# The gate by pairs of batches: tiles of 128 tokens, contractions of 128 rows, and its weights split in the MLP

## The chip, the cores and the metric

One core of one Trainium2 chip runs the whole program. The metric is device time in microseconds of one execution, given as the median of several. The core has a matrix engine (TensorE, PE here; PEld is its weight load), VectorE (DVE), ScalarE (ACT), GpSimd (POOL), and SyncE (SP), which issues most DMAs. Each engine runs its instructions in the order in which they were written.

## The reference

Three parts, in float32, with 4 batches, 448 tokens, 12 heads of 64, model width 768:

```python
x = attention(rmsnorm(q), rmsnorm(k), v)            # [4, 448, 768]
x = x + relu(layernorm(x) * g @ w_ch1) @ w_ch2      # hidden width 3072
h = relu(x @ w_in)                                  # [4, 448, 1024]
u, v = h[..., :512], h[..., 512:]
v_n = (v - mean(v)) / sqrt(var(v) + 1e-6)
v_s = einsum('ts,bsd->btd', w_spatial, v_n) + b_spatial[None, :, None]
out = (u * v_s) @ w_out                             # [4, 448, 768]
```

The last five lines are "the gate" below; `w_spatial` is 448x448.

## The kernel before

Large products are made in three float32r matmuls: each operand is split into a rounded part (`hi`) and the rest (`lo`), and `THREE` names the pairs hi*hi, hi*lo, lo*hi. A split costs one copy (ACT or DVE) and one subtraction (POOL or DVE).

Each part of the kernel first lists its operations with `op(n, engine, us, fn, r, w, new)`: an intended place `n`, an estimate of the time, what is read and written, and the ring of buffers that is used. `arrange` then plays the list through with these estimates and writes the instructions out in the order in which they would start; that order is fixed at build time.

Attention comes first. Then the MLP runs 24 slices `u` of the hidden width over 4 batches: `ph` (18 matmuls), `pm` (18 matmuls), the latter one step behind; ACT and DVE make `h` from `ph`, DVE adds `pm` to `y`. The slices' weights come as 64-bit numbers into a raw slot (`wraw`), are converted to float32 into `wc` by ACT and four DVE operations (`plan_conv`), and split by ACT and POOL into `ws` (`plan_parts`). Between them stand sixteen "gate" pieces: `w_in` and `w_out` are converted in the same way, and stored to DRAM from `wc` as plain float32 (`win_dram`, `wout_dram`).

The gate follows at about 999 us, batch by batch, in `plan_gate`:

- `gv`: per batch four tiles of 112 tokens, each 18 matmuls that stream 512 columns of the weights of v against the tokens of `ys` (the split input). ACT applies relu, DVE takes mean and variance, makes the reciprocal root in eleven small steps for all four tiles (`rsqrt_steps`), scales and rounds; POOL makes the rest (`gvs`).
- `gu`: four groups of 128 columns of u, 18 matmuls each over 448 tokens.
- `gs`: four groups, each contracting over the 448 tokens in four tiles of 112 rows, 12 matmuls.
- DVE adds the bias and multiplies by u, ACT and POOL split the result (`gg`).
- `gp`, after each second batch (`plan_out`): 14 row tiles of 128 in two halves of 12 matmuls, copied by ACT (`go`) and stored.

The gate's weights are loaded and split there: v's at the MLP's end (`plan_win`), u's and `w_out` in the first batch; `w_spatial` is loaded, transposed by PE in 16 small matmuls (`psp`) and split. The inputs of batches 1 to 3 go through DRAM (`y_dram`), since `ys` has one buffer.

Of the kernel before, what the change touches and what calls it, by code (L numbers as in the profile page):

```python
# [34 lines left out]
def f32(ap):  # L35
    return ap.bitcast(F32)
# [3 lines left out]
def attention_mlp_gated(ctx, tc, q, k, v, g_q, g_k, g_ln, w1, w2, w_in, w_sp, b_sp, w_out, out):  # L40
# [19 lines left out]
    win_dram = dram.tile([DM, 2 * DG], F32, name="win_dram")  # L60
    wout_dram = dram.tile([DG, DM], F32, name="wout_dram")
# [5 lines left out]
    gl_c = const.tile([P, NK], F32, name="gl_c")  # L67


    def rsqrt_steps(y, t, a):  # L70
# [13 lines left out]
        return steps  # L84

# [80 lines left out]
    def plan_parts(i, n, since=()):  # L166
# [15 lines left out]
        if kind == "gate":  # L182
            dma(n, src.shape[1] / 2, lambda: nc.sync.dma_start(u, pl["c"]), r=[c])
# [10 lines left out]
    TURN = 0.19  # L194

# [592 lines left out]
    def plan_gate(gp, W, ys, b, n):  # L788

        st = {}  # L790
        vn, uu = {}, {}
        cols = slice(b % 2 * S, (b % 2 + 1) * S)
        yr = [f"ys{b}_{kk}" for kk in range(NK)]

        def v_pe(c):
            pv = st["pv", c] = ps["s"].tile([P, 512], F32, tag="s", name=f"gv{b}_{c}")
            for kk in range(NK):
                for m, (a, e) in enumerate(THREE):
                    nc.tensor.matmul(  # L799
                        pv[:CP, :],  # L800
                        ys[b][:, a, kk, c * CP : (c + 1) * CP],
                        W["v", kk][:, e],
# [4 lines left out]
        def v_act(c):  # L807
            vn[c] = gp["vr"].tile([CP, DG], F32, tag="vr", name=f"vr{b}_{c}")
            nc.scalar.activation(vn[c], st["pv", c][:CP, :], AF.Relu)

        def v_stats(c):
            if c == 0:
                st["mv"] = gp["small"].tile([CP, NCH, 2], F32, tag="gmv", name=f"gmv{b}")
            s6 = gp["small"].tile([CP, 6], F32, tag="g6", name=f"g6{b}_{c}")
            nc.vector.bn_stats(s6, vn[c])
            nc.vector.bn_aggr(st["mv"][:, c], s6)

        def v_rstd(z):
# [14 lines left out]

        def v_hi(c):
            if c == 0:
                st["vs"] = gp["vs"].tile([CP, NCH, 2, DG], F32R, tag="xn", name=f"gvs{b}")
            nc.vector.tensor_copy(st["vs"][:, c, 0], vn[c])

        def v_lo(c):
            nc.gpsimd.tensor_tensor(st["vs"][:, c, 1], vn[c], f32(st["vs"][:, c, 0]), op=ALU.subtract)  # L840

        for c in range(NCH):
            o = f"{b}_{c}"
            op(n, "PE", 3.84, lambda c=c: v_pe(c), r=yr + [f"win_v{kk}" for kk in range(NK)], w=["gv" + o], new="s")
            op(n + 1, "ACT", 0.48, lambda c=c: v_act(c), r=["gv" + o], w=["vr" + o], new="vr")
            op(n + 1, "DVE", 0.7, lambda c=c: v_stats(c), r=["vr" + o], w=["mv" + o])
        for z in range(11):
            op(n + 3, "DVE", 0.07, lambda z=z: v_rstd(z), r=[f"mv{b}_{c}" for c in range(NCH)], w=[f"rstd{b}"])
        for c in range(NCH):
            o = f"{b}_{c}"  # L850
            op(n + 4, "DVE", 0.34, lambda c=c: v_norm(c), r=[f"rstd{b}"], w=["vr" + o])
            if c == 0:
                op(n + 4, "DVE", 0.34, lambda: v_hi(0), r=["vr" + o], w=[f"vs{b}", "vs" + o], new="vs")
            else:
                op(n + 4, "DVE", 0.34, lambda c=c: v_hi(c), r=["vr" + o, f"vs{b}"], w=["vs" + o])
            op(n + 4, "POOL", 1.23, lambda c=c: v_lo(c), r=["vr" + o, f"vs{b}"], w=["vs" + o])

        def u_pe(g):
            pu = st["pu", g] = ps["t"].tile([P, 512], F32, tag="t", name=f"gu{b}_{g}")
            for kk in range(NK):  # L860
                for m, (a, e) in enumerate(THREE):
                    nc.tensor.matmul(  # L862
                        pu[:, :S],
                        W["u", kk][:, a, g * P : (g + 1) * P],
                        ys[b][:, e, kk, :],
                        start=(kk == 0 and m == 0),
                        stop=(kk == NK - 1 and m == 2),
                    )

        def u_act(g):  # L870
            uu[g] = gp["u"].tile([P, S], F32, tag="gu", name=f"u{b}_{g}")
            nc.scalar.activation(uu[g], st["pu", g][:, :S], AF.Relu)

        for g in range(NG):
            o = f"{b}_{g}"
            op(n + 8, "PE", 3.37, lambda g=g: u_pe(g), r=yr + [f"win_u{kk}" for kk in range(NK)], w=["gu" + o], new="t")
            op(n + 9, "ACT", 0.424, lambda g=g: u_act(g), r=["gu" + o], w=["u" + o], new="u")

        def s_pe(g):
            pg = st["pg", g] = ps["o"].tile([P, 512], F32, tag="o", name=f"gs{b}_{g}")  # L880
            for c in range(NCH):
                for m, (a, e) in enumerate(THREE):
                    nc.tensor.matmul(  # L883
                        pg[:, :S],
                        st["vs"][:, c, a, g * P : (g + 1) * P],
                        W["sp"][:, e, c, :],
                        start=(c == 0 and m == 0),
                        stop=(c == NCH - 1 and m == 2),
                    )

        def s_add(g):
            st["t", g] = gp["t"].tile([P, S], F32, tag="gt", name=f"gt{b}_{g}")
            nc.vector.tensor_tensor(
                st["t", g], st["pg", g][:, :S], W["b"].rearrange("p c i -> p (c i)"), op=ALU.add
            )

        def s_gate(g):
            nc.vector.tensor_tensor(st["t", g], st["t", g], uu[g], op=ALU.mult)

        def s_hi(g):  # L900
            if b % 2 == 0:
                gt[g] = gp["g"].tile([P, 2, 2 * S], F32R, tag="gg", name=f"gg{b}_{g}")
            act_copy(gt[g][:, 0, cols], st["t", g])

        def s_lo(g):
            eng = nc.vector if b == B - 1 else nc.gpsimd
            eng.tensor_tensor(gt[g][:, 1, cols], st["t", g], f32(gt[g][:, 0, cols]), op=ALU.subtract)

        for g in range(NG):
            o = f"{b}_{g}"  # L910
            r = [f"vs{b}"] + [f"vs{b}_{c}" for c in range(NCH)] + [f"wsp{c}" for c in range(NCH)]
            op(n + 16, "PE", 2.25, lambda g=g: s_pe(g), r=r, w=["gs" + o], new="o")
            op(n + 17, "DVE", 0.535, lambda g=g: s_add(g), r=["gs" + o, "bsp"], w=["gt" + o], new="gt")
            op(n + 17, "DVE", 0.535, lambda g=g: s_gate(g), r=["u" + o], w=["gt" + o])
            both = f"gg{b // 2 * 2}_{g}"
            r, w, new = (["gt" + o, both], [f"gg{b}_{g}_"], None) if b % 2 else (["gt" + o], [both, f"gg{b}_{g}_"], "gg")
            op(n + 17, "ACT", 0.46, lambda g=g: s_hi(g), r=r, w=w, new=new)
# [361 lines left out]
```

## Time and profile before

| | |
|---|---|
| median of 3 runs | 1229.29 us (1228.19 to 1230.41) |
| the profiled execution | 1229.24 us |
| its span | 1227.5 us |
| PE busy | 1198.8 us, 98% of the span |
| DVE, ACT, POOL busy | 794.9, 451.3, 325.1 us |
| MLP and gate | about 302 to 999 us, and 999 to 1224 us |

Busy times are means over stages with different limits. A stage is read from its chain of waits: the pieces of work that ended last there, in order of time, each released by the one before it. Times inside the trace count from the start of the span.

### The profile page before, as it was taken

The numbers are of one execution on the slowest core, as the hardware profiler recorded it, in microseconds if no ns is written. First come the engines' busy times: TensorE is split into PE (matmuls) and PEld (weight loads), VectorE is DVE, ScalarE is ACT, GpSimd is POOL, SyncE is SP. The second block draws the span as 40 slices with busy tenths as digits, with TensorE's granted clock in tenths as the row PEclk, the third lists the DMA queues.
The fourth block names the chain that finished last, engine by engine and source line by source line (L and its number), as shares of the span: only waits on it lengthen the run. The fifth ranks groups of instructions, "written<-read, shape, count | busy, mean of one in ns | idle before, by whom it ended". The sixth has DMA issues, their size and how long they took to land.

```text
span 1227.5 us, 16696 instructions
## 1 busy us (share of the span) xinstructions
PE 1198.8 (98%) x6528; PEld 1020.5 (83%) x6528; DVE 794.9 (65%) x1436; ACT 451.3 (37%) x910; POOL 325.1 (26%) x266
## 2 busy tenths in 40 slices
PE   3999999999999999999999999999999999999998
PEld 1556656566899999999999999999999989889898
DVE  5889998977898656464747484855535578452250
ACT  2888888887422212131212122221212222122112
POOL 4764767525111102020202011110201115212120
PEclk9999999999999999999999999999999999999999
DMA  4312112111214231231313141402100063011103
GB/s 100 80 54 77 53 46 73 61 42 42 77 54 153 69 104 54 101 93 62 112 44 112 52 156 51 154 26 78 53 26 26 26 227 113 23 46 52 39 1 90
DMA packets 50861, 89.00 MB, mean 73 GB/s; under 512 B 3952, under 2 KB 39152, under 8 KB 50016
## 3 DMA queue, kind: packets, MB, share of 16 engines
q1 hardware_dynamic: 50352, 83.82, 22.5%
q10 hardware_dynamic: 432, 4.13, 0.8%
q8 instruction: 51, 0.84, 0.3%
q14 instruction: 26, 0.21, 0.1%
HBM read 73.58 MB, written 14.35 MB: 72 GB/s over the span
## 4 chain that ended last, share of the span: by engine, by line
PE 89%; DVE 7%; DMA 2%; ACT 1%; issue 0%; POOL 0%; SPq 0%; DVEq 0%
PE ph L705 28%; PE pm L728 28%; PE s L475 5%; PE gp L930 5%; PE gu L862 5%; PE gv L799 4%; PE po L525 4%; PE t L508 4%; PE gs L883 3%; DVE nmx L481 2%; DMA win_ru<-win_dram 1%; PE pk L452 1%; PE pq L452 1%; PE pxT L580 1%; DVE PT L518 1%; PE px L559 1%
## 5 line engine op out<-in xcount | busy, mean ns | idle before, releaser
L728 PE MATMUL pm<-h,ws 128*128 128x448 f32 x1728 | 361.6, 362 | 0.0
L705 PE MATMUL ph<-xn,ws 128*128 128x448 f32 x1728 | 361.1, 362 | 0.0
L728 PEld LDWEIGHTS pm<-h,ws 128*128 128x128 f32 x1728 | 323.7, 187 | 22.4 <-issue 0.7
L705 PEld LDWEIGHTS ph<-xn,ws 128*128 128x128 f32 x1728 | 323.8, 187 | 21.8 <-DVE y L736 0.2
L180 POOL TENSOR_TENSOR ws<-wc,ws 128x768 fp32r<-128x768 f32 x48 | 96.5, 2009 | 574.8 <-ACT ws L101 561.9
L736 DVE TENSOR_TENSOR y<-pm,y 128x448 f32<-128x448 f32 x318 | 175.9, 613 | 76.7 <-PE pm L728 76.7
L715 ACT ACTIVATE h<-ph 128x448 fp32r<-128x448 f32 x96 | 51.9, 541 | 267.1 <-PE ph L705 259.7
L720 DVE SCALAR_TENSOR_TENSOR h<-ph,h 128x448 fp32r<-128x448 f32 x96 | 59.5, 620 | 125.7 <-ACT h L715 124.6
L485 ACT ACTIVATE P<-s,nmx 112x448 f32<-112x448 f32 x192 | 119.2, 635 | 30.7 <-DVE nmx L481 30.4
L481 DVE TENSOR_REDUCE nmx<-s 112x2 f32<-112x896 f32 x96 | 101.0, 1080 | 18.7 <-PE s L475 18.1
L91 ACT ACTIVATE wc<-wr 128x768 f32<-128x768 f32 (+1 forms) x64 | 55.2, 865 | 139.3 <-POOL ws L180 45.8
L475 PE MATMUL s<-kT,qT 64*112 64x448 f32 x384 | 88.3, 581 | 0.6 <-ACT qT L461 0.6
L508 PE MATMUL t<-ident,P 112*112 112x112 f32 x768 | 85.4, 260 | 1.7 <-ACT P L485 1.0
L101 ACT ACTIVATE ws<-wc 128x768 fp32r<-128x768 f32 x48 | 40.6, 845 | 113.1 <-PE ph L705 97.2
L508 PEld LDWEIGHTS t<-ident,P 112*112 112x112 f32 x768 | 75.9, 133 | 5.0 <-ACT P L485 4.1
L525 PE MATMUL po<-PT,vr 112*64 112x448 f32 x384 | 77.5, 545 | 0.0
L94 DVE SCALAR_TENSOR_TENSOR wc<-wr,wc 128x768 int32<-128x768 int32 (+1 forms) x64 | 69.2, 1081 | 1.6
L95 DVE SCALAR_TENSOR_TENSOR wc<-wr,wc 128x768 uint32<-128x768 uint32 (+1 forms) x64 | 67.6, 1057 | 1.1
L92 DVE TENSOR_SCALAR wc<-wc 128x768 f32<-128x768 f32 (+1 forms) x64 | 37.6, 587 | 46.3 <-ACT wc L91 46.3
L799 PE MATMUL gv<-winv,ys 128*112 128x512 f32 x288 | 67.2, 393 | 0.0
L475 PEld LDWEIGHTS s<-kT,qT 64*112 64x112 f32 x384 | 31.5, 179 | 41.6 <-issue 23.4
L525 PEld LDWEIGHTS po<-PT,vr 112*64 112x64 f32 x384 | 25.4, 136 | 48.5 <-issue 38.4
(167 smaller groups left out, 1267.5 us busy)
## 6 DMA issues: line engine op xcount, KB each, us to landing
wr<-in_moe_w_ch_dram SPq DMA_DIRECT2D x48, 768.0 KB, 4.4
wr<-in_moe_w_in_dram SPq DMA_DIRECT2D x12, 512.0 KB, 3.8
vr<-in_v_dram SPq DMA_DIRECT2D x24, 224.0 KB, 2.7
kr<-in_k_dram SPq DMA_DIRECT2D x11, 448.0 KB, 4.0
qr<-in_q_dram SPq DMA_DIRECT2D x11, 448.0 KB, 4.5
y_dram<-y ACTq DMA_DIRECT2D x3, 1344.0 KB, 9.0
yl<-y_dram SPq DMA_DIRECT2D x3, 1344.0 KB, 7.2
win_dram<-wc SPq DMA_DIRECT2D x12, 256.0 KB, 4.7
```

The lines of the kernel that those rows point to most:

```text
L94: lambda: v.scalar_tensor_tensor(ci, hi, -0x40000000, ci, op0=ALU.bitwise_and, op1=ALU.bitwise_or),
L95: lambda: v.scalar_tensor_tensor(cu, lo.bitcast(U32), 29, cu, op0=ALU.logical_shift_right, op1=ALU.bitwise_or),
L180: nc.gpsimd.tensor_tensor(t[:, 1], pl["c"], f32(t[:, 0]), op=ALU.subtract)
L475: nc.tensor.matmul(p[:CP, j, :S], pr["qT"][rows, c * CP : (c + 1) * CP], pr["kT"][rows], start=True, stop=True)
L481: nc.vector.tensor_reduce(t, pr["s", c][:CP, :, :S], axis=AX.X, op=ALU.max, negate=True)
L485: nc.scalar.activation(t, pr["s", c][:CP, j, :S], AF.Exp, bias=pr["m", c][:, j : j + 1], scale=1.0, accum_out=pr["sum"][:, j, c : c + 1],)
L508: nc.tensor.transpose(p[:CP, e, c * CP : (c + 1) * CP], pr["P", j, c][:, kc * CP : (kc + 1) * CP], ident[:CP, :CP])
L525: nc.tensor.matmul(pr["po"][j * D : (j + 1) * D, :S], raw["v", i][:, j, kc, :], pr["PT", kc // 2, j][:, kc % 2], start=(kc == 0), stop=(kc ...
L705: nc.tensor.matmul(hid[u, b][0][:, :S], s1[:, a, kk, :], xn[b][:, c, kk, :], start=(kk == 0 and m == 0), stop=(kk == NK - 1 and m == 2),)
L728: nc.tensor.matmul(po[:, :S], s2[:, a, m * P : (m + 1) * P], hs[:, c, :], start=(first and e == 0), stop=(last and e == 2),)
L736: nc.vector.tensor_tensor(y[b][:, m, :], po[:, :S], y[b][:, m, :], op=ALU.add)
L799: nc.tensor.matmul(pv[:CP, :], ys[b][:, a, kk, c * CP : (c + 1) * CP], W["v", kk][:, e], start=(kk == 0 and m == 0), stop=(kk == NK - 1 an ...
```

## The change

- The gate works by pairs of batches. The tokens of a pair are cut into seven tiles of 128: three whole ones of each batch, and one that holds the last 64 tokens of both (`plan_mixed` copies these beside one another). `gv` has seven tiles per pair.
- `gs` contracts over three tiles of 128 rows and one half tile of 64. In "joint" groups the half tiles of both batches follow one another by turns (`s_half`), on rows 0 to 63 and 64 to 127, into banks of different pools. The last group of the second pair is done batch by batch.
- The reciprocal root is made per tile by two POOL operations (`rsqrt`: add, power).
- The gate's weights are split in the MLP: a gate piece is now rounded by ACT and subtracted by DVE into its own raw slot, and both parts are stored (`split_out`). `w_spatial` becomes four more pieces (`sp`), transposed by DVE. The gate loads split weights and does nothing more to them.
- `ys0` and `ys1` are both made at the MLP's end; only batches 2 and 3 go through DRAM.
- The tiles of u's weights and of the split v start 48 elements into their slots. The order is v, u, u, s of the first pair; three v tiles and u of batch 2; `gp` of the first pair; four v tiles, u, s and `gp` of the second.

```diff
+    def rsqrt(y, a, eps):
+        nc.gpsimd.tensor_scalar(a, a, eps, None, op0=ALU.add)
+        nc.gpsimd.tensor_tensor(y, a, half_c[: a.shape[0]].to_broadcast(list(a.shape)), op=ALU.pow)
...
+        if 4 <= u < 4 + 2 * NCH:
+            pieces.append(("sp", u // 2 - 2, None))
...
+        op(n, "ACT", 0.73 * f / DM, hi, r=[f"wc{i}"], w=[f"wr{i}"])
+        op(n, "DVE", 0.88 * f / DM, lo, r=[f"wc{i}"], w=[f"wr{i}"])
+        dma(n + 1, f, store, r=[f"wr{i}"])
...
+        dma(n_load, 229, load, w=[f"wr{i}"], new=f"wraw{half}")
+        op(n, "DVE", 0.55, turn, r=[f"wr{i}"], w=[f"wc{i}"], new=f"wc{half}")
+        split_out(i, n + 1, pl, S, wsp_dram[P * t : min(P * (t + 1), S)], True)
...
         if kind == "gate":
-            dma(n, src.shape[1] / 2, lambda: nc.sync.dma_start(u, pl["c"]), r=[c])
+            split_out(i, n, pl, src.shape[1], u)
...
+        def s_full(e, g):
+            s_tile(e, g)
+            for c in range(3):
+                for m, (a, k) in enumerate(THREE):
+                    nc.tensor.matmul(
+                        st["pg", e, g],
+                        st["vs"][:, 4 * e + c, a, g * P : (g + 1) * P],
+                        W["sp"][:, k, c],
+                        start=(c == 0 and m == 0),
+                        stop=False,
+                    )
+
+        def s_half(es, g):
+            for m, (a, k) in enumerate(THREE):
+                for e in es:
+                    rows = slice(e * 64, (e + 1) * 64)
+                    nc.tensor.matmul(
+                        st["pg", e, g], st["vs"][rows, 3, a, g * P : (g + 1) * P], W["sp"][rows, k, 3],
+                        start=False, stop=(m == 2),
+                    )
...
+            if joint(g):
+                op(m, "NONE", 0, lambda: None, r=r, w=[f"gs{b0}_{g}"], new="o")
+                op(m, "PE", 4.5, lambda g=g: s_pe((0, 1), g), r=r, w=[f"gs{b0 + 1}_{g}", f"gs{b0}_{g}"], new="g")
+            else:
+                for e in range(2):
+                    op(m, "PE", 2.5, lambda e=e, g=g: s_pe((e,), g), r=r, w=[f"gs{b0 + e}_{g}"], new="og"[e])
...
+                act_copy(mixed[pair][:, :, :, half], f32(ys[b][:, :, :, 3 * P :]))
...
-        for c in range(NCH):
-            op(c, "PE", 0.38, lambda c=c: sp_pe(c), r=["spr"], w=[f"psp{c}"], new="o")
...
+        plan_gate(gp, W, ys, mixed, 0, 0, {"v": range(7), "u": (8, 12), "s": 16})
+        plan_ys(2, 14, 1)
+        plan_mixed(2, 20)
+        plan_ys(3, 46, 1)
+        plan_mixed(3, 52)
+        plan_gate(gp, W, ys, mixed, 1, 40, {"v": (0, 1, 2, 15, 16, 17, 18), "u": (4, 20), "s": 26})
+        plan_out(gp, W, 0, 40 + 9)
+        plan_out(gp, W, 2, 40 + 40)
```

## Rows read from the trace of the kernel before

**Rows 1.** The page: busy us, share, instructions; groups with busy us, mean ns.

```profile
PE 1198.8 (98%) x6528; PEld 1020.5 (83%) x6528; DVE 794.9 (65%) x1436; ACT 451.3 (37%) x910; POOL 325.1 (26%) x266
...
L728 PE MATMUL pm<-h,ws 128*128 128x448 f32 x1728 | 361.6, 362 | 0.0
...
L728 PEld LDWEIGHTS pm<-h,ws 128*128 128x128 f32 x1728 | 323.7, 187 | 22.4 <-issue 0.7
...
L481 DVE TENSOR_REDUCE nmx<-s 112x2 f32<-112x896 f32 x96 | 101.0, 1080 | 18.7 <-PE s L475 18.1
...
L475 PE MATMUL s<-kT,qT 64*112 64x448 f32 x384 | 88.3, 581 | 0.6 <-ACT qT L461 0.6
```

**Rows 2.** The chain, gate's first batch: start us, length us, work.

```profile
1012.89 0.65 PE psp L1199 x4
...
1017.71 1.27 PE psp L1199 x12
```

**Rows 3.** Timeline of PE, same stretch: start, length, work, idle time before it.

```profile
1012.89 0.65 PE L1199 MATMUL psp<-ident,wsp_r 112*112 112x112 f32 x4 [1.07 <-DVE g L815]
```

**Rows 4.** The chain, gate's later batches.

```profile
1083.88 16.55 PE gv L799 x72
1100.42 14.40 PE gu L862 x72
...
1184.62 9.71 PE gs L883 x48
1194.33 29.15 PE gp L930 x168
```

**Rows 5.** Timeline of PE in the attention, 200 to 216 us.

```profile
206.47 1.01 PE L475 MATMUL s<-kT,qT 64*112 64x448 f32 x4
207.41 0.60 PE L452 MATMUL pk<-ident,kq 112*128 112x112 f32 x4
...
210.53 1.74 PE L508 MATMUL t<-ident,P 112*112 112x112 f32 x16 [0.16 <-ACT P L485]
212.11 0.55 PE L580 MATMUL pxT<-ident,x 112*128 112x112 f32 x4
212.59 2.51 PE L475 MATMUL s<-kT,qT 64*112 64x448 f32 x12
215.03 1.35 PE L525 MATMUL po<-PT,vr 112*64 112x448 f32 x6
```

**Rows 6.** Timeline of weight loads in the attention.

```profile
201.34 0.18 PEld L475 LDWEIGHTS s<-kT,qT 64*112 64x112 f32 x2 [0.20 <-ACT PT L101]
```

**Rows 7.** Stretches: busy PE, PEld, DVE, ACT, POOL (instructions), PEclk, DMA share, GB/s.

```profile
400.00:520.00 120.00, 120.00 (x601) 112.48 (x601) 71.48 (x115) 25.28 (x37) 16.99 (x8) 1.00 0.26 84
...
999.20:1012.00 12.80, 12.62 (x55) 9.23 (x53) 5.21 (x10) 4.46 (x9) 0.00 (x0) 1.00 1.01 385
```

**Rows 8.** Timeline of ACT in the MLP.

```profile
486.13 0.67 ACT L91 ACTIVATE wc<-wr 128x512 f32<-128x512 f32 x1 [4.03 <-DMA win_dram<-wc]
...
498.08 0.90 ACT L91 ACTIVATE wc<-wr 128x768 f32<-128x768 f32 x1 [2.12 <-DMA win_dram<-wc]
...
531.41 0.85 ACT L101 ACTIVATE ws<-wc 128x768 fp32r<-128x768 f32 x1 [3.40 <-PE ph L705]
```

**Rows 9.** The chain in the MLP.

```profile
545.78 3.60 PE pm L728 x18
549.38 3.60 PE ph L705 x18
```

**Rows 10.** DMA issues, 420 to 920 us: count, KB each, median us to landing.

```profile
wr<-in_moe_w_ch_dram SPq DMA_DIRECT2D x35, 768.0 KB, 4.4
...
win_dram<-wc SPq DMA_DIRECT2D x10, 256.0 KB, 5.4
```

**Rows 11.** Groups by shape: busy us, mean ns, idle us before.

```profile
L840 POOL TENSOR_TENSOR gvs<-vr,gvs 112x512 fp32r<-112x512 f32 x16 | 25.0, 1593 | 56.9 <-DVE gvs L837 56.9
...
L353 POOL TENSOR_TENSOR sq0k<-sq0k 112x256 f32<-112x256 f32 x1 | 0.7, 716 | 0.1
...
L893 DVE TENSOR_TENSOR gt<-gs,bsp 128x448 f32<-128x448 f32 x16 | 10.0, 623 | 40.7 <-PE gs L883 40.6
```

More of the change, by code (lines that the diff above doesn't have):

```diff
@@ L194, in attention_mlp_gated @@
     TURN = 0.19
+    LATE = {"PE": 0.29, "ACT": 0.1, "DVE": 0.08, "POOL": 0.08, "SP": 2.4, "SPA": 2.4, "NONE": 0}
     ORDER = "po-1 s3+1 pk+2 t11 pq+2 t01 px-1 t00 t10 pxT-2 s0+1 s2+1 s1+2".split()
@@ L786, in attention_mlp_gated, with plan_gate, source, held @@
     gt = {}
-    def plan_gate(gp, W, ys, b, n):
+    def plan_gate(gp, W, ys, mixed, pair, n, at):
         st = {}
[L791 to L796, printed above, removed]
+        uu = {}
+        b0 = 2 * pair
+        tiles = 2 * S // P
+        joint = lambda g: pair == 0 or g < NG - 1
+        def source(t):
+            if t == 3:
+                return mixed[pair]
+            return ys[b0 + t // 4][:, :, :, t % 4 * P : (t % 4 + 1) * P]
+        def held(t):
+            if t == 3:
+                return [f"mx{pair}"] + [f"mx{pair}_{e}" for e in range(2)]
+            b = b0 + t // 4
+            return [f"ysp{b}"] + [f"ys{b}_{kk}" for kk in range(NK)]
+        def v_pe(t):
+            pv = st["pv", t] = ps["g"].tile([P, 512], F32, tag="g", name=f"gv{pair}_{t}")
+            of = source(t)
             for kk in range(NK):
@@ new lines, in v_rstd, with v_norm, v_hi @@
+        def v_rstd(t):
+            st["r", t] = gp["small"].tile([P, 1], F32, tag="grstd", name=f"grstd{pair}_{t}")
+            rsqrt(st["r", t], st["mv", t][:, 1:2], EPS)
+        def v_norm(t):
+            v = st["v", t]
+            nc.vector.tensor_scalar(v, v, st["mv", t][:, 0:1], st["r", t], op0=ALU.subtract, op1=ALU.mult)
+        def v_hi(t):
+            if t == 0:
+                st["vs"] = gp["vs"].tile([P, tiles * 2 * DG + 64], F32R, tag="vs", name=f"gvs{pair}")[
+                    :, 48 : 48 + tiles * 2 * DG
+                ].rearrange("p (t a f) -> p t a f", t=tiles, a=2)
+            nc.vector.tensor_copy(st["vs"][:, t, 0], st["v", t])
@@ new lines, in v_lo @@
+        def v_lo(t):
+            nc.gpsimd.tensor_tensor(st["vs"][:, t, 1], st["v", t], f32(st["vs"][:, t, 0]), op=ALU.subtract)
+        wv = [f"win_v{kk}" for kk in range(NK)]
+        for t in range(tiles):
+            o, m = f"{pair}_{t}", n + at["v"][t]
+            op(m, "PE", 4.14, lambda t=t: v_pe(t), r=held(t) + wv, w=["gv" + o], new="g")
+            op(m + 1, "ACT", 0.48, lambda t=t: v_act(t), r=["gv" + o], w=["vr" + o], new="vr")
+            op(m + 1, "DVE", 0.7, lambda t=t: v_stats(t), r=["vr" + o], w=["mv" + o], new="mv")
+            op(m + 1, "POOL", 0.6, lambda t=t: v_rstd(t), w=["mv" + o])
+            op(m + 1, "DVE", 0.34, lambda t=t: v_norm(t), r=["mv" + o], w=["vr" + o])
+            w, new = ([f"vs{pair}"], "vs") if t == 0 else ([], None)
+            op(m + 1, "DVE", 0.34, lambda t=t: v_hi(t), r=["vr" + o] + ([] if t == 0 else [f"vs{pair}"]), w=w + ["vs" + o], new=new)
+            op(m + 1, "POOL", 1.23, lambda t=t: v_lo(t), r=["vr" + o, f"vs{pair}"], w=["vs" + o])
@@ L803, in v_pe, with u_pe @@
+        def u_pe(e, g):
+            pu = st["pu", e, g] = ps["g"].tile([P, 512], F32, tag="g", name=f"gu{b0 + e}_{g}")
+            for kk in range(NK):
+                for m, (a, c) in enumerate(THREE):
+                    nc.tensor.matmul(
+                        pu[:, :S],
+                        W["u"][:, kk, a, g * P : (g + 1) * P],
+                        ys[b0 + e][:, c, kk, :],
                         start=(kk == 0 and m == 0),
@@ L834, in v_hi @@
[L834 to L840, printed above, removed]
-        for c in range(NCH):
[L843 to L889, printed above, removed]
@@ L905, in s_lo, with u_act @@
[L905 to L917, printed above, removed]
-            op(n + 17, *(("DVE", 0.53) if b == B - 1 else ("POOL", 1.08)), lambda g=g: s_lo(g), r=["gt" + o, both], w=[f"gg{b}_{g}_"])
+        def u_act(e, g):
+            uu[e, g] = gp["u"].tile([P, S], F32, tag="gu", name=f"u{b0 + e}_{g}")
+            nc.scalar.activation(uu[e, g], st["pu", e, g][:, :S], AF.Relu)
@@ new lines, in plan_gate, with s_tile @@
+        for e in range(2):
+            for g in range(NG):
+                o, m = f"{b0 + e}_{g}", n + at["u"][e] + g
+                r = [f"ysp{b0 + e}"] + [f"ys{b0 + e}_{kk}" for kk in range(NK)] + [f"win_u{kk}" for kk in range(NK)]
+                op(m, "PE", 3.6, lambda e=e, g=g: u_pe(e, g), r=r, w=["gu" + o], new="g")
+                op(m + 1, "ACT", 0.45, lambda e=e, g=g: u_act(e, g), r=["gu" + o], w=["u" + o], new="u")
+        def s_tile(e, g):
+            pl = "og"[e]
+            st["pg", e, g] = ps[pl].tile([P, 512], F32, tag=pl, name=f"gs{b0 + e}_{g}")[:, :S]
@@ new lines, in s_lo, with place, place_last @@
+        def s_lo(e, g):
+            cols = slice(e * S, (e + 1) * S)
+            eng = nc.vector if pair else nc.gpsimd
+            eng.tensor_tensor(gt[g][:, 1, cols], st["t", e, g], f32(gt[g][:, 0, cols]), op=ALU.subtract)
+        def place():
+            t = gp["gg3"].tile([P, 3, 2, 2 * S], F32R, tag="xn", name=f"gg{pair}")
+            for g in range(3):
+                gt[g] = t[:, g]
+        def place_last():
+            gt[NG - 1] = gp["g"].tile([P, 2, 2 * S], F32R, tag="gg", name=f"gg{pair}_3")
@@ L1043, in attention_mlp_gated @@
              "PT": 5, "OT": 2, "xs": 2, "nmx": 4, "rs": 2, "ssum": 3, "ln": 1, "lnx": 6, "s": 3, "x": 2},
-            24, {"PE": 0.29, "ACT": 0.1, "DVE": 0.08, "POOL": 0.08, "SP": 2.4, "SPA": 2.4, "NONE": 0}, 0.05,
+            24, LATE, 0.05,
         )
@@ new lines, in plan_ys, with place, load, of @@
+        def plan_ys(b, n, step, src=None):
+            pair, e = divmod(b, 2)
+            yl = {}
+            def place():
+                ys[b] = (xn_b if b == 1 else xn_a).tile([P, 2, NK, S], F32R, tag="xn", name=f"ys{b}")
+            def load(h):
+                yl[h] = gp["yl"].tile([P, NK // 2, S], F32, tag="yl", name=f"yl{b}_{h}")
+                nc.sync.dma_start(yl[h], y_dram[b][:, h * NK // 2 : (h + 1) * NK // 2])
+            def of(kk):
+                return src[:, kk] if src is not None else yl[kk // 3][:, kk % 3]
@@ new lines, in lo @@
+                nc.vector.tensor_tensor(ys[b][:, 1, kk], of(kk), f32(ys[b][:, 0, kk]), op=ALU.subtract)
+            old = [f"xn{b}_{m}" for m in range(NK)] if b < 2 else []
+            op(n, "NONE", 0, place, w=[f"ysp{b}"] + old, new="ysB" if b == 1 else "ysA")
+            if src is None:
+                for h in range(2):
+                    dma(n + h, 688, lambda h=h: load(h), r=[f"yd{b}"], w=[f"yl{b}_{h}"], new="yl")
+            for kk in range(NK):
+                m, r = n + step * kk, [f"ysp{b}"] + ([f"y{b}_{kk}"] if src is not None else [f"yl{b}_{kk // 3}"])
+                op(m, "ACT", 0.46, lambda kk=kk: hi(kk), r=r, w=[f"ys{b}_{kk}"])
+                op(m, "DVE", 0.535, lambda kk=kk: lo(kk), r=r, w=[f"ys{b}_{kk}"])
@@ new lines, in plan_mixed, with place, copy @@
+        def plan_mixed(b, n):
+            pair, e = divmod(b, 2)
+            def place():
+                mixed[pair] = gp["mx"].tile([P, 2, NK, P], F32R, tag="mx", name=f"ysm{pair}")
+            def copy():
+                half = slice(e * 64, (e + 1) * 64)
+                act_copy(mixed[pair][:, :, :, half], f32(ys[b][:, :, :, 3 * P :]))
+            if e == 0:
+                op(n, "NONE", 0, place, w=[f"mx{pair}"], new="mx")
+            r = [f"mx{pair}", f"ysp{b}"] + [f"ys{b}_{kk}" for kk in range(NK)]
+            op(n, "ACT", 0.9, copy, r=r, w=[f"mx{pair}_{e}"])
@@ L1144, in attention_mlp_gated @@
             {"ln": 1, "lnx": 6, **bufs}, 20,
-            {"PE": 0.29, "ACT": 0.1, "DVE": 0.08, "POOL": 0.08, "SP": 2.4, "SPA": 2.4, "NONE": 0}, 0.05,
+            LATE, 0.05,
         )
@@ L1152, in attention_mlp_gated @@
         plan_last(28)
-        plan_win(l1, 1, "v", lambda sh, nm: wpools["raw"][0].tile(sh, F32, tag="wraw", name=nm), "wraw0", 0)
-        plan_ys(0, lambda: y[0], 14, 1)
-        for b in range(1, B):
+        plan_win(l1, 1, "v", 0)
+        for b in range(2):
+            plan_ys(b, 14 + 7 * b, 1, y[b])
+        for b in range(2, B):
             op(
@@ new lines, in attention_mlp_gated @@
+        plan_win(gp["w"], 0, "u", 0)
+        W["b"] = gp["w"].tile([P, S], F32, name="bsp")
+        W["sp"] = gp["w"].tile([P, 2, NCH, S], F32R, name="wsp_s")
+        W["out"] = gp["w"].tile([P, NG, 2, DM], F32R, name="wout")
+        def load_sp():
+            tokens = wsp_dram.rearrange("(i c) f -> c i f", c=NCH)
+            for t in range(NCH):
+                for base in (0, 64) if t == NCH - 1 else (0,):
+                    j, last = P * t, min(P * (t + 1), S)
+                    while j < last:
+                        c, i = divmod(j, CP)
+                        m = min(CP - i, last - j)
+                        at = base + j - P * t
+                        nc.sync.dma_start(
+                            f32(W["sp"][at : at + m, :, t]), tokens[c, i : i + m].rearrange("i (a s) -> i a s", a=2)
+                        )
+                        j += m
@@ L1190, in attention_mlp_gated @@
         op(
-            8, "DVE", 0.53, lambda: nc.vector.tensor_copy(W["b"], st["br"].rearrange("p (i c) -> p c i", c=NCH)),
+            8, "DVE", 0.53, lambda: nc.vector.tensor_copy(W["b"], raw_b["t"].rearrange("p (i c) -> p c i", c=NCH)),
             r=["br"], w=["bsp"],
         )
-        def sp_pe(c2):
-            p = st["p", c2] = ps["o"].tile([P, 512], F32, tag="o", name=f"psp{c2}")
-            rows = st["spr"].rearrange("p c (i e) -> p c e i", e=NCH)
-            for c in range(NCH):
-                nc.tensor.transpose(p[:CP, c * CP : (c + 1) * CP], rows[:, c, c2, :], ident[:CP, :CP])
```

245 lines of the change are left out of this document (114 added, 131 removed).

## Prediction

> **What bounds the kernel now.** I read the table of busy times first: TensorE (PE) is busy for 98% of the span [rows 1]. It is the bound, so an edit is worth what it takes off PE's own stream, and work on VectorE (DVE), ScalarE (ACT), GpSimd (POOL) or the queues is worth nothing unless PE waits for it.
>
> Next the chain that ended last, for the gate alone, which is where the diff sits. From about 999 us to 1223.48 the chain is PE piece after PE piece [rows 2, 4]; the reader should see in its starts and lengths that a piece begins where the one before it ends. The timeline of PE shows the one hole: 1.07 us ahead of the first transposes of the spatial weights, which queue ahead of the fourth `gv` tile [rows 3]. So the gate is some 224 us of matmuls, and the change is to be costed in matmul pitches. From [rows 4]: `gv` (512 columns) 16.55 / 72 = 0.2299 us each, `gu` (448 columns) 14.40 / 72 = 0.2000, `gs` 9.71 / 48 = 0.2023, `gp` (384 columns) 29.15 / 168 = 0.1735. The granted clock reads 1.00, its upper level, in the stretches of [rows 7].
>
> The profiled execution took 1229.24 us around a span of 1227.5; the median of the runs is 1229.29. The sum is made on 1229.24.
>
> **v in tiles of 128 tokens.** Before, 4 batches x 4 tiles x 18 = 288 `gv` matmuls, each streaming 512 columns against 112 tokens. After, two pairs x 7 tiles x 18 = 252. The columns streamed stay 512, so I keep the pitch: 36 x 0.2299 = **-8.28 us**. Bound on the other side: from `gp` to `gu`, 64 more columns cost 0.0265 us, which would put 512 columns at 0.2265; the 0.0034 lost against that may come from the 112-token tiles. If it goes, 252 x 0.0034 = 0.9 us more is gained.
>
> TensorE: Matmul & The Clock Gate, of the Trainium skill, section "Back-to-back issue gap", gives N/2.4 + 2.5 ns, which is 0.216 us at 512 columns; the trace disagrees with its 0.2299. By the page the term would be 7.8 instead of 8.3 us, and I go by the trace.
>
> **Spatial weights.** Their 16 transposes leave PE: 0.65 + 1.27 us [rows 2], and with them the hole of 1.07 [rows 3]: **-2.99 us**. They become four `sp` pieces in the MLP, transposed by DVE.
>
> **s with contractions of 128 rows.** Before, 192 `gs` matmuls of 112 rows, 38.84 us. After, a batch is three full tiles (9 matmuls) and a half tile of 64 rows (3). In a joint group the halves of the two batches alternate between rows 0-63 and 64-127, and write different banks. If the two run at once, a joint group is 18 + 3 = 21 pitches instead of 24; seven groups of the eight are joint.
>
> Do they run at once? The attention's `s` matmuls are of 64 rows and alternate likewise. A record of `s` lasts 581 ns against 362 for `pm` [rows 1], of which 200 is pitch (18 in 3.60 us [rows 9]); so some 0.16 us of a record is latency and an `s` streams for about 0.42. Yet from 212.59 to 215.03 there are 12 of them, from 206.47 to 207.41 there are 4: eight more cost 1.50 us, 0.1875 each [rows 5]. Two overlap. Two loads of 64-row weights also lie within 0.18 us [rows 6], where one of `pm` takes 0.187 [rows 1].
>
> What the switch of row form costs is in [rows 5] too. Four `s` cost 4 x 0.1875 = 0.75 us but `pk` starts 0.94 after them: 0.19 to leave. Sixteen `t` transposes take 1.58 us, 0.099 each; four `pxT` from 212.11 should end at 212.51 and `s` starts at 212.59: 0.09 to enter. So 0.28 us per visit, and there are nine visits (seven joint, two in the split last group).
>
> Sum: 7 x (21 x 0.2023 + 0.28) + 2 x (12 x 0.2023 + 0.28) = 37.1 us, **-1.7 us**. Bounds: free switches, 171 x 0.2023 = 34.6, -4.2; halves that don't overlap, 192 pitches and the visits, +2.5. I take -1.7, since the rows that it uses are of the same form.
>
> **u and out** keep 288 and 336 matmuls: 0. Fewer hidden splits on DVE and POOL in the gate are worth 0 too.
>
> **New order of the gate.** `ys0` is split at the MLP's end as before; `ys1` now too, six DVE subtractions of 0.62 [rows 11], 3.7 us, that can stand ahead of the last `h`, which has 5.8 us of slack (worked out below). Seven `gv` tiles (29 us) then cover the loads of u's weights (3.1 MB) and of the split spatial weights (1.8 MB): DMA moved 385 GB/s there before [rows 7], so these with the two remaining `y` stores (2.8 MB) need about 20 us from 992. `ys2` and `ys3` load behind `gu` and `gp`. At s of the second pair, `gl` of the last group ends after DVE's six operations of the joint group before it (6 x 0.6 [rows 11]) and four steps of its own (2.4). That is 3.6 + 2.4 - 2.7 (the split group's first half) = 3.3 us behind that half, while the other half takes 2.7 and the first nine `gp` matmuls, which read the other three groups, 1.56. I take 0; if `gp` waited for all four groups, 0.6 to 0.9.
>
> **POOL's new square root.** Add and power on a 128x1 column, 14 times, are shown nowhere. Nearest row: 112x256 in 0.72 us on POOL [rows 11]; two of them 1.4 us above, 0 below. Cover: of the second pair's last four tiles the first is evicted 3 x 4.14 + 14.40 = 26.8 us before s, less some 3 of the chain: 24 us for four, each of which also needs the 1.59 us of `gvs` on POOL [rows 11], so 24 / 4 - 1.6 = 4.4 us per tile are free. Cost 0.
>
> **Pieces in the MLP.** Sixteen gate pieces gain an ACT copy, a DVE subtraction and twice the store, and four `sp` pieces are new: a load, a DVE transpose, the split and a store. DVE is busy for 71 of 120 us there [rows 7], and one loop of 57.6 us (sixteen pieces of 3.60 [rows 9]) gains about 4 us. DVE's transpose is shown nowhere: 0 below, above it the 1.08 us of a 112x896 reduction [rows 1], hidden either way. A raw slot is now held until its store lands: 256 KB took 5.4 us and the next load 4.4 [rows 10]. Cover: `w2` is converted at 498.08 but split only at 531.41, when its slot is free, and read by PE at 545.78 [rows 8, 9]. What can hurt is ACT queued on a late load with `h` behind it. ACT stood 4.03 us on a store ahead of 486.13 [rows 8] and PE lost nothing, for `h` has 7.2 us (one `pm`, one `ph`, 3.60 each [rows 9]) and needs about 1.4 (an ACT and a DVE operation of 0.6 and their hand-overs): 5.8 us of slack. Cost 0.
>
> **Sum.** 1229.24 - 8.28 - 2.99 - 1.7 = **1216.3 us**. Of the likeliest case with its bounds: 1212.9 (0.9 more in v, free switches, rounding) to 1217.2.
>
> **The rivals.**
>
> *Halves as dear as full matmuls.* Either they don't overlap: s costs 38.84 + 2.5, and the time is 1229.24 - 8.28 - 2.99 + 2.5 = 1220.5. Or each second and third half-load stands open behind the first, since it goes to the same rows: with the first one, 7 x 3 loads of 0.187 us [rows 1], 3.9 us, 1220.2. For it: none of the rows has fp32r matmuls of 64 rows with 128-column weights. Against it: [rows 5, 6], and `pm`, which loads the same 128 rows each time, hides its 0.187 in a pitch of 0.2000. Chance 0.13 for both.
>
> The second way is a rule of TensorE: Matmul & The Clock Gate, of the Trainium skill, section "The mechanism": a weight load overlaps matmuls in flight only when it goes to other rows of the array. By that rule the loads of `pm` would stand open too; the trace does not agree.
>
> *The MLP loses its cover, and the result is slower.* Each of eight loops has stores that hold a raw slot; ACT waits for the load behind one of them, and `h` stands behind ACT. It decides from a wait of 5.8 + 13 / 8 = 7.4 us in each loop. Twice the store is twice 4.03, 8.1 us: 8 x 2.3 = 18 us lost, 1234.7. Against it: conversion runs 33 us ahead of the split [rows 8], so a load that is late by 4 us has room if ACT takes it up later. Chance 0.06; a mild form, 0.5 us per loop, gives 1220.3, chance 0.07.
>
> *POOL's power is slow.* At more than 4.4 us per tile the second s waits; the first has (6 x 4.14 + 2 x 14.40 - 3) / 7 - 1.6 = 5.6 free per tile, so that from 6.3 us on (4 x 1.9 + 7 x 0.7 = 12.5) nearly the whole gain is gone. The nearest rows are far below. Chance 0.04, 1229 or more.
>
> *Switches free.* 1213.7; chance 0.10.
>
> **How the numbers follow.** The forecast has 0.60. About 0.2%, 2.5 us, is what a measurement tells from no change. The mild cases all stay under 1226.8: faster 0.60 + 0.13 + 0.07 + 0.10, less 0.01 for mishaps among them: 0.89. Slower takes the two bad cases, 0.08, since a part of them ends within 0.2%: 0.03. The range, 1212.5 to 1221.5 us, holds the forecast, free switches and dear halves with the 0.9 of the last wait.
>
> **What would show it.** Right: `gv` x252 at 0.230; no transposes in the gate; s pieces of about 18.1 us for the first pair and 19.0 for the second; `gu` and `gp` as before; gate some 211 us from the last `pm`; MLP pieces of 3.60 without holes. Wrong: holes ahead of `ph` or `pm` released by ACT or DVE; a joint group at 5.1 us instead of 4.5; `gs` released by POOL; a wait of `gu` for its weights.

## The result, and the profile after

The changed kernel takes 1216.57 us (median of 4, 1216.25 to 1217.94) against 1229.06 us before (4 runs, 1228.19 to 1230.41): a ratio of 0.9903, 95% interval 0.989 to 0.9917. The prediction was 1216.3 us.

The profiled execution took 1216.79 us around a span of 1215.0. The chain that ended last, from the MLP's end on (start us, length us, work), answers to [rows 2, 4]:

```profile
988.01 3.61 PE ph L765 x18
...
992.91 6.57 DVE y L796 x12
999.49 0.04 issue
999.53 28.86 PE gv L872 x126
1028.39 28.80 PE gu L920 x144
1057.19 4.08 PE gv L872 x18
1061.27 3.60 PE gs L947 x18
1064.87 0.81 PE gs L959 x6
1065.68 3.80 PE gs L947 x18
...
1079.52 8.39 PE gv L872 x36
...
1131.45 16.36 PE gv L872 x72
1147.81 14.40 PE gu L920 x72
1162.21 3.60 PE gs L947 x18
...
1180.67 0.81 PE gs L959 x3
1181.48 29.34 PE gp L1026 x168
1210.82 0.02 issue
```

The reader should see two things. The gate is again a row of PE pieces that touch. And just ahead of it the chain leaves PE for DVE's additions to `y`, which it did not before. The view of what PE waited for, from 302 us to 1000 us, has one entry in the changed kernel:

```profile
PE gv L872 <- DVE y L796: 0.7, 1, 0.7
```

So the MLP, with all its new pieces, has no wait of PE at all. From the end of the last `pm` (7.2 us after `ph`: 999.39 before, 998.82 after) to the end of `gp` the gate took 224.09 us and takes 212.00. Summed from the chains' pieces:

| | before | after | difference | predicted |
|---|---|---|---|---|
| `gv` | 66.36 | 57.69 | -8.67 | -8.28 |
| transposes of the spatial weights, hole ahead of them | 2.99 | 0 | -2.99 | -2.99 |
| `gs` | 38.84 | 37.52 | -1.32 | -1.7 |
| `gu`, `gp` | 115.92 | 116.08 | +0.16 | 0 |
| hole ahead of the first `gv` | 0 | 0.71 | +0.71 | 0 |
| gate | 224.09 | 212.00 | -12.09 | -12.97 |

The profiled times differ by 12.45 us: these 12.09, another 0.57 ahead of the gate, and 0.2 us more behind it. In the chain the first `s` begins 0.4 us earlier, at 16.45 us, and the first `ph` 0.6 us earlier, both in the attention, which the change leaves alone but for one more POOL fill and a small constant tile. In the profiles of the experiments, which share all this, the last `pm` ends anywhere from 998.1 to 999.8 us.

### The profile page after: what moved, and what is told of

Its sections match the earlier page's. It is cut to its first block, busy times and chain, and to the rows that moved or that the text cites. A ratio compares the mean times of both kernels' runs of the same rounds, so it can differ in the third digit from the quotient of the medians.

```text
span 1215.0 us, 16606 instructions
## 1 busy us (share of the span) xinstructions
PE 1186.9 (98%) x6476; PEld 1010.4 (83%) x6476; DVE 774.5 (64%) x1398; ACT 459.2 (38%) x916; POOL 304.9 (25%) x279
## 4 chain that ended last, share of the span: by engine, by line
PE 90%; DVE 8%; ACT 1%; DMA 0%; issue 0%; POOL 0%; SPq 0%; DVEq 0%; ACTq 0%
PE ph L765 28%; PE pm L788 28%; PE s L535 5%; PE gp L1026 5%; PE gv L872 5%; PE gu L920 5%; PE po L585 4%; PE t L568 4%; DVE nmx L541 2%; PE gs L947 2%; PE pk L512 1%; PE gs L959 1%; PE pq L512 1%; PE pxT L640 1%; DVE PT L578 1%; PE px L619 1%
## 5 line engine op out<-in xcount | busy, mean ns | idle before, releaser
L239 POOL TENSOR_TENSOR ws<-wc,ws 128x768 fp32r<-128x768 f32 x48 | 92.4, 1925 | 578.9 <-ACT ws L109 553.2
L100 DVE TENSOR_SCALAR wc<-wc 128x768 f32<-128x768 f32 (+1 forms) x64 | 41.0, 645 | 50.3 <-ACT wc L99 49.9
L102 DVE SCALAR_TENSOR_TENSOR wc<-wr,wc 128x768 int32<-128x768 int32 (+1 forms) x64 | 64.5, 1011 | 1.5
L103 DVE SCALAR_TENSOR_TENSOR wc<-wr,wc 128x768 uint32<-128x768 uint32 (+1 forms) x64 | 63.2, 988 | 1.6
L109 ACT ACTIVATE PT<-t 112x896 f32<-112x896 f32 x72 | 62.1, 931 | 1.4 <-PE t L568 1.4
```

The lines of the kernel that those rows point to most:

```text
L102: lambda: v.scalar_tensor_tensor(ci, hi, -0x40000000, ci, op0=ALU.bitwise_and, op1=ALU.bitwise_or),
L103: lambda: v.scalar_tensor_tensor(cu, lo.bitcast(U32), 29, cu, op0=ALU.logical_shift_right, op1=ALU.bitwise_or),
L109: nc.scalar.activation(d, s, AF.Copy)
L239: nc.gpsimd.tensor_tensor(t[:, 1], pl["c"], f32(t[:, 0]), op=ALU.subtract)
```

## The experiments

All edits are to the changed kernel, unless the text says that it is the kernel before. Where no range is given, there is one run. They ran on three chips, with the kernel before beside them: it took 1228.52 us (median of 7) beside the first four, 1228.73 (one run) beside the tiles of 128, the standing bank and the slower root, and 1228.56 (median of 7) beside "Other tokens" and "Both improvements".

**Halves next to one another.** The halves of neighbouring groups are joined, and those of the last group, which did not overlap, now do; the 64-row form is visited four times instead of nine.

```diff
...
+            if g % 2 and es != (1,):
+                s_half((0, 1), g, True)
             for e in es:
-                s_full(e, g)
-            s_half(es, g)
+                s_full(e, g, g % 2 == 0)
+            if g % 2 == 0:
+                s_half(es, g, False)
...
```

> The half matmuls of two neighbouring groups of gs stand next to one another (full, half | half, full), and those of the split last group follow those of the joint group before it, both batches by turns. Visits to the 64-row form fall from nine to four. Mine: a visit costs about 0.41 us in the changed kernel (0.81 us for six halves against 0.60 of streaming, and 0.20 more on the next full group), so 5 x 0.41 = 2.05 us go, and 3 x 0.20 because the last group's halves now overlap: about 1213.9 us, pieces of 12 halves of about 1.41 us. Rival: the extra is a cost of each half matmul and not of the visit; then 12 halves take 1.6 us, only the 0.6 of the last group goes, 1216.0.

Measured: 1213.75 us (1213.43 to 1214.59), ratio 0.9879 (0.9863 to 0.9896). The chain of the first pair's s:

```profile
1060.51 3.60 PE gs L946 x18
1064.12 1.41 PE gs L958 x12
1065.53 7.41 PE gs L946 x36
1072.94 1.41 PE gs L958 x12
1074.36 3.81 PE gs L946 x18
1078.17 8.16 PE gv L872 x36
```

Twelve halves take 1.41 us: six pitches of 0.20 and 0.21. The extra belongs to the visit and is paid once on entering, and once more, 0.20, on the next full piece (7.41 instead of 7.20; a `gv` piece straight behind halves took 8.39, here 8.16). The rival, a price on each half, is out.

**No joint groups.**

```diff
-        joint = lambda g: pair == 0 or g < NG - 1
+        joint = lambda g: False
```

> All groups of gs are done batch by batch, so that no two half matmuls of different batches stand by turns. Mine (halves of two batches overlap): each of seven groups gains three pitches of 0.20 and one visit of 0.41, +7.1 us, about 1223.7. Rival (the halves of a joint group do not overlap): only the visits, +2.9 us, about 1219.4.

Measured: 1224.56 us in one run. In its chain three halves alone take as long as six did:

```profile
1061.86 1.80 PE gs L947 x9
1063.66 0.80 PE gs L959 x3
1064.47 2.01 PE gs L947 x9
1066.48 0.81 PE gs L959 x3
```

Both pairs' s take 22.35 us each, 44.70 in all against 37.52: +7.2 us, as expected (the rest of the +8.0 is an MLP that ends later in this profile). Halves of two batches overlap; the rival "halves as dear as full matmuls" is out.

**The halves batch by batch.**

```diff
-            for m, (a, k) in enumerate(THREE):
-                for e in es:
+            for e in es:
+                for m, (a, k) in enumerate(THREE):
```

> In a joint group the three halves of the first batch come first, then the three of the second, instead of by turns. Mine: PE starts matmuls in order, so only the last of the first batch and the first of the second overlap; a piece of six halves takes about five pitches instead of three, 1.21 us instead of 0.81, +2.8 us in all, about 1219.4. Rivals: the two row halves run on by themselves, and the piece stays at 0.81; or the turns matter for nothing because halves never overlap, and it stays at 0.81 too (the run without joint groups tells these apart).

Measured: 1216.25 us. My expectation failed: the first two pieces of six are 0.82 and 0.81 us long, as with turns. The view of this line within one such piece (count, then shortest, median and longest ns, then first and last start) shows where they stand:

```profile
L959 PEld LDWEIGHTS gs<-wsp_s,gvs x6: 183/185/188, 1064.2 to 1064.6; 64*128 64x128 f32 x6
L959 PE MATMUL gs<-wsp_s,gvs x6: 361/364/471, 1064.2 to 1064.8; 64*128 64x448 f32 x6
```

All six matmuls start within 0.6 us although they stand as three and three. Three on the same rows take 0.80 us alone (the run without joint groups), so those that run at once are of different batches. If a later one could not start before an earlier one, the second batch's first half would start with the first batch's third, 0.4 us in, and the last one 0.8 us in. By these times, PE's matmuls do not wait for one another in the order in which they were written when they go to different row halves: that each engine runs its instructions in the order in which they were written holds with this exception. TensorE: Matmul & The Clock Gate, of the Trainium skill, section "The mechanism", says that matmuls keep program order in their starts and ends; by that rule the piece would take 1.2 us, and this trace does not agree.

**No shift in the slots.**

```diff
-                    :, 48 : 48 + tiles * 2 * DG
+                    :, 0 : tiles * 2 * DG
...
-                        :, at : at + NK * 2 * DG
+                        :, 0 : NK * 2 * DG
```

> The tiles of u's weights and of the split v start at the beginning of their slots instead of 48 elements in. If the shift is what brought the pitch of gs from 0.2023 to 0.2000 us, gs returns to 0.2023 (18 in 3.64 us) and the time rises by about 0.4 us; if gu needs it as well, by up to 0.7 more. Rival: the pitch of 0.2023 came from contractions of 112 rows, and nothing changes.

Measured: 1218.27 us. The gate from the first `gv` on is 1.14 us longer than in the changed kernel, close to the 0.4 + 0.7 expected:

```profile
1028.69 29.18 PE gu L920 x144
...
1061.99 3.65 PE gs L947 x18
1065.63 0.81 PE gs L959 x6
```

`gu` goes from 0.2000 to 0.2026 us per matmul. The first full piece of `gs` takes 3.65 us instead of 3.60, the later ones 0.02 to 0.05 more, together 0.3 us in 144 matmuls: about 0.2020. The old 0.2023 of `gs` thus needs no 112 rows; where these weights begin in their slot sets some 1% of the pitch.

**Tiles of 128 tokens in the kernel before.** Three of four `gv` tiles take 128 tokens.

```diff
-                        pv[:CP, :],
-                        ys[b][:, a, kk, c * CP : (c + 1) * CP],
+                        pv[: P if c < 3 else CP, :],
+                        ys[b][:, a, kk, c * CP : c * CP + (P if c < 3 else CP)],
```

> The kernel before, in which three of the four gv tiles of a batch take 128 tokens instead of 112 (16 of them again in the next tile; the rows beyond 112 are not used). If the pitch of 0.2299 us came from 112-column weights, these 216 matmuls run at about 0.2267 and the kernel is 0.7 us faster although it computes more. Rival: the pitch belongs to the place of the data or to 512 columns, and the time stays.

Measured: 1228.17 us, beside 1228.73 for the kernel before. The difference is not a gain in `gv`: its 72 matmuls take 16.61, 16.61 and 16.58 us in the last three batches, where the kernel before has 16.66, 16.55 and 16.55:

```profile
1041.97 16.61 PE gv L799 x72
```

The width of the weights alone does not set the pitch.

**Other tokens, before and after.** In the kernel before, `gv` tiles of 112 tokens begin at 0, 128 and 256; in the changed kernel the whole tiles begin at 48, 176 and 304. The first leaves tokens 112 to 127 and 240 to 255 out of v, the second tokens 0 to 47.

```diff
-                        ys[b][:, a, kk, c * CP : (c + 1) * CP],
+                        ys[b][:, a, kk, (c * P if c < 3 else c * CP) : (c * P if c < 3 else c * CP) + CP],
...
-            return ys[b0 + t // 4][:, :, :, t % 4 * P : (t % 4 + 1) * P]
+            return ys[b0 + t // 4][:, :, :, t % 4 * P + 48 : (t % 4 + 1) * P + 48]
```

> The kernel before, with three of the four gv tiles of a batch reading tokens from 0, 128 and 256 on instead of 0, 112 and 224, still 112 of them (the tokens are the wrong ones, so the output is not the reference's). If the pitch of 0.2299 us comes from weights that begin at odd places (multiples of 448 bytes), tiles of 4.15 us become 4.08, and the gate is about 0.6 us faster. Rival: something else than the place in the slot (the bank, the streamed weights of v) sets it, and the tiles stay at 4.15.

> The changed kernel, with the whole tiles of gv reading tokens from 48, 176 and 304 on instead of 0, 128 and 256 (the wrong tokens again; the mixed tile stays as it is). If the place of the weights sets the pitch, the six whole tiles of a pair go from 4.08 to about 4.15 us, +0.8 us in all. Rival: they stay at 4.08.

Measured: 1228.86 us and 1217.23 us, each within 0.6 of its own kernel, so the tiles must be read one by one. ACT copies each `gv` tile as soon as it is done, so the starts of these copies in the timeline of ACT give the length of a tile. Kernel before, last batch:

```profile
1157.93 0.60 ACT L809 ACTIVATE vr<-gv 112x512 f32<-112x512 f32 x1 [2.19 <-PE gv L799]
1162.08 0.60 ACT L809 ACTIVATE vr<-gv 112x512 f32<-112x512 f32 x1 [3.55 <-PE gv L799]
1166.24 0.60 ACT L809 ACTIVATE vr<-gv 112x512 f32<-112x512 f32 x1 [3.57 <-PE gv L799]
1170.32 0.60 ACT L809 ACTIVATE vr<-gv 112x512 f32<-112x512 f32 x1 [3.48 <-PE gv L799]
```

The changed kernel, the same view of the second pair:

```profile
1135.67 0.60 ACT L878 ACTIVATE vr<-gv 128x512 f32<-128x512 f32 x1 [3.69 <-PE gv L872]
1139.75 0.60 ACT L878 ACTIVATE vr<-gv 128x512 f32<-128x512 f32 x1 [3.48 <-PE gv L872]
1143.83 0.60 ACT L878 ACTIVATE vr<-gv 128x512 f32<-128x512 f32 x1 [3.48 <-PE gv L872]
```

The second, third and fourth tile took 4.15, 4.16 and 4.08 us before; a whole tile takes 4.08 after (0.2267 per matmul), and a mixed one 4.14. With the tokens moved, those before became 4.12, 4.12 and 4.17, and the whole ones after 4.12 (0.2289). The chain of the last batch, or of the second pair's last four tiles, in the two runs:

```profile
1153.13 16.57 PE gv L799 x72
...
1131.77 16.48 PE gv L872 x72
```

In the changed kernel these four tiles took 16.36 us, and over all twelve tiles that were moved the difference is 0.46 us: there the place of the tokens is worth about 0.04 us per tile, half of what I expected. In the kernel before, two tiles gained 0.03 to 0.04 us, but the last one, which was not moved, lost 0.09, and the batch takes 16.57 us beside 16.55. So where a tile begins does not by itself explain why `gv` was slower there; neither does its width. The cause stays open.

**The first tile in a standing bank.**

```diff
+        bank_of = lambda t: "o" if pair == 0 and t == 0 else "g"
...
-            pv = st["pv", t] = ps["g"].tile([P, 512], F32, tag="g", name=f"gv{pair}_{t}")
+            pv = st["pv", t] = ps[bank_of(t)].tile([P, 512], F32, tag=bank_of(t), name=f"gv{pair}_{t}")
```

> The changed kernel with the first gv tile in a bank of the pool that is there all along, and not in the pool of five banks that takes the place of the MLP's banks. Mine: the hole of 0.72 us ahead of the first gv, which DVE's last addition to y ends, comes from that pool, and goes: about 1215.9. Rival: gv waits for something else that is late then (the split of ys1, the weights), and the hole stays.

Measured: 1215.51 us, and the chain goes from `pm` straight into `gv`:

```profile
991.35 7.20 PE pm L788 x36
998.55 28.58 PE gv L874 x126
```

The hole came from the pool of five banks, which takes the place of the MLP's pools and waits for the last reader in them. In the kernel before, the first `gv` had a pool of two banks and started at 999.21, while DVE's additions, in its timeline there, were still running:

```profile
994.08 5.96 DVE L736 TENSOR_TENSOR y<-pm,y 128x448 f32<-128x448 f32 x11
```

The hole cost more than its 0.71 us: the seven `gv` tiles behind it take 28.86 us, here 28.58. From the end of the last `pm` to the end of `gp` the standing bank gives 0.98 us.

**A slower root.** The power of each tile is done seven or thirteen times.

```diff
-        nc.gpsimd.tensor_tensor(y, a, half_c[: a.shape[0]].to_broadcast(list(a.shape)), op=ALU.pow)
+        for _ in range(7):
+            nc.gpsimd.tensor_tensor(y, a, half_c[: a.shape[0]].to_broadcast(list(a.shape)), op=ALU.pow)
```

> The power on POOL is done seven times over for each tile, with the same result: 6 x 0.6 = 3.6 us more per tile, 4.4 in all with the addition. By the prediction 4.4 us per tile are free, so the time changes by less than 1 us. Rival: a chain through DVE, which waits for the root with other work behind it, makes PE wait earlier; then the time rises by several us.

> The power done thirteen times over: 12 x 0.6 = 7.2 us more per tile, 8.0 in all. By the prediction s of the second pair then waits 4 x 3.6 = 14 us, and s of the first 7 x 2.4 = 17; the fill with a tile of v between them may hide some: 1230 to 1247 us. Rival: the reserve is larger than was worked out, and the time rises by less than 10 us.

Measured: 1221.34 and 1267.22 us, both beyond what I expected. POOL's timeline of the second pair, seven powers:

```profile
1147.11 1.29 POOL L903 TENSOR_TENSOR gvs<-vr,gvs 128x512 fp32r<-128x512 f32 x1 [1.12 <-DVE gvs L900]
1148.49 0.22 POOL L91 TENSOR_SCALAR gmv<-gmv 128x1 f32<-128x1 f32 x1
1148.80 4.34 POOL L93 TENSOR_TENSOR grstd<-gmv,half_c 128x1 f32<-128x1 f32 x7
1154.27 1.31 POOL L903 TENSOR_TENSOR gvs<-vr,gvs 128x512 fp32r<-128x512 f32 x1 [1.13 <-DVE gvs L900]
```

A tile takes POOL 7.15 us here and not the 6.0 reckoned with (4.4 and the 1.6 of `gvs`), since 1.12 of each are a wait for DVE, which scales and rounds between the root and `gvs`. And a second path, the rival's: the waits of the same run, in all, times, longest:

```profile
ACT vr L879 <- POOL gvs L903: 13.1, 2, 6.8
...
PE gv L873 <- ACT ys L110: 2.9, 1, 2.9
```

ACT waits for a `vr` buffer that POOL holds, with the split of `ys2` behind it; the next pair's first `gv` is 2.9 us late. Behind that wait PE is slower too, as its timeline and a stretch around it show (PE, PEld, DVE, ACT, POOL busy, granted clock, DMA share, GB/s):

```profile
1061.64 3.65 PE L873 MATMUL gv<-winv,ys 128*128 128x512 f32 x9 [2.93 <-ACT ys L110]
...
1061.00:1065.00 4.00, 3.36 (x9) 2.65 (x10) 1.79 (x3) 3.23 (x7) 0.00 (x0) 0.57 0.14 15
```

Nine matmuls take 0.41 us each instead of 0.23. The granted clock is 1.00 (2.4 GHz) in the whole gate of the changed kernel; after PE had stood for 2.93 us it has a mean of 0.57 here, mostly the lower level of 1.2 GHz. This wait of 2.9 us, one of 0.3 for POOL's `gvs` in the second pair, and the 1.6 lost at the lower clock make the 4.8 us of the rise. With thirteen powers the same path gives

```profile
PE gv L873 <- DVE ys L1193: 14.8, 1, 14.8
PE gs L948 <- DVE gvs L900: 12.9, 2, 8.8
PE gu L921 <- ACT vr L879: 7.2, 1, 7.2
```

All waits of PE in this gate make 39.2 us, 38.5 more than in the changed kernel, and the time rises by 50.65. Most of the rest is slower matmuls: PE is busy in the gate for 222.2 us instead of 211.3. From 1200 to 1215 us, around waits of 4.1 and 8.8 us, the granted clock has a mean of 0.53, and the six halves at 1214.74 take 1.42 us instead of 0.81.

**Both improvements.** The joined halves and the standing bank together, and the changed kernel as it is beside them.

> The changed kernel with neighbouring halves and with the first gv tile in the standing bank. The two act at different places, so their gains should add: 2.8 us and 0.7 to 1.0 us below the changed kernel, about 1212.9. Rival: the earlier start of gv only moves the wait to the next thing that is late (a copy, a weight), and 1213.7 stays.

> The changed kernel unaltered, on the same chip as the run before it: about 1216.5 by either theory; it gives the difference to the version with both edits on one chip.

Measured: 1213.14 us (1212.88 to 1213.66), ratio 0.9875 (0.9859 to 0.9891), and 1216.66 us (1216.39 to 1216.75), ratio 0.9902 (0.9887 to 0.9917). The gains add, 3.5 us; no wait of PE is left from 320 us on. This is the fastest version here.

## Why the prediction was right

**What bounds it.** Right, and the base of the rest: PE's pieces touch in both chains, so pitches could be counted.

**v.** The count of 36 matmuls was right. The pitch fell too, to 0.2267, which the prediction had as its bound (0.2265, 0.9 us) and not as its value. The table's -8.67 hides part of this: its 57.69 us hold 0.3 of the first tile behind the wait and 0.2 of a tile behind the halves; without these v gave 9.2, not 8.28. The guess that the 112-token width was the cause is not borne out (the tiles of 128 in the kernel before). Where a tile begins in its slot is worth 0.04 us per tile in the changed kernel, but moving the tiles gained nothing over a batch in the kernel before; why the pitch was higher there is open. The formula that the prediction set beside this pitch is given in the Trainium skill, TensorE: Matmul & The Clock Gate, section "Back-to-back issue gap", for an isolated matmul, not for a stream of them.

**Spatial weights.** -2.99 us, as the sum had it.

**s.** The overlap of halves is shown, by 1224.56 us without it. Two sizes were off and partly cancel. A visit costs 0.41 us, not the 0.28 of the attention's rows: nine visits, some 1.2 us more, of which 0.4 appear on the `gv` and `gp` pieces that follow. And full matmuls run at 0.2000, not 0.2023, because of the shift: 171 x 0.0023 = 0.4 us less. With the 0.4 on other pieces s gave 0.9 us, not the 1.7 forecast. The Trainium skill, TensorEngine Tiling (Array Packing), section "Key Properties", says that a change of tiling mode drains the engine; the trace agrees in so far as the change has a price here, 0.21 us going in and 0.20 coming out.

**New order of the gate.** One thing was missed: 0.71 us ahead of `gv`, about 1.0 with the slower first tile behind it. I looked for a late operand there and put the price at 0; it was the banks. The wait at the last `gp` that I had bounded at 0.9 did not come: `gp` follows at once, longer by the 0.20 of the visit. u's weights landed in time.

**POOL's root.** Its price is 0.22 + 0.57 us per tile, within the bounds, and costs PE nothing. The cover of 4.4 us per tile was mis-sized: it left out DVE's step between the root and `gvs`, ACT's wait for a buffer, and the lower clock behind a wait of PE. With the 0.79 us measured this did not show.

**The MLP.** No wait there, as forecast. The stretch that answers to the first of [rows 7] (PE, PEld, DVE, ACT, POOL busy, clock, DMA share, GB/s):

```profile
400.00:520.00 120.00, 120.00 (x602) 112.47 (x601) 75.44 (x127) 30.17 (x44) 15.01 (x8) 1.00 0.34 112
```

DVE gained 4.0 and ACT 4.9 us in 120. In a loop of 57.6 us that is 1.9 and 2.3, so the 4 us that the prediction gave a loop fit both engines together, not DVE alone. The stores, feared to take twice as long, did not (below).

The sum was nearly exact partly by luck. Inside the gate v gave 0.9 us more than forecast and s 0.8 less, and the wait that was missed cost 1.0; together the gate gave 0.9 us less. A start that was 0.6 us earlier, for which nothing in the change is shown to be the cause, covers most of that.

## What to carry to other kernels

Where one engine's pieces touch, count its instructions and take each pitch from the chain; a wait that the rows don't show is then looked for at each place where buffers or banks change hands, not only where operands are made. Half-height matmuls pay if two of different rows can overlap, and if many of them stand together, since the change of form costs two matmul pitches per visit. When slack is worked out for an engine, the other engines' steps inside its chain belong in the sum; and past the slack a wait of PE can cost more than its length, since the matmuls behind it ran at the lower clock here.

## What had not been expected of the hardware

- Matmuls on different row halves overlap even when they don't stand by turns: six in 0.82 us.
- A wait of PE can be followed by matmuls at the lower clock: behind one of 2.93 us nine of them took 0.41 us each instead of 0.23.
- A tile of u's weights that begins 48 elements into its slot instead of 0 runs at 0.2000 us per matmul instead of 0.2026.
- A store of twice the size landed sooner. DMA issues from 420 to 920 us of the changed kernel, beside [rows 10], where 256 KB took 5.4 us. They now go to whole rows of their own tensor, but this alone cannot be the cause: the stores of `w_out` went to whole rows before as well, 384 KB in 5.5 us, and now land, 768 KB, in 3.2. The cause stays open:

```profile
win_dram<-wr SPq DMA_DIRECT2D x10, 512.0 KB, 2.6
```
